# A routing kernel's experts' logits: the rows as stationary operand, and the gate's product in plain float32 in three groups of columns

## The chip, the cores and the metric

The kernel runs on one core of a Trainium2 chip. The metric is the device time of one execution in microseconds (us); each time shown is that of whole executions, and the profile is one further execution. TensorE is called PE in the profile, its weight loads PEld; VectorE is DVE, ScalarE is ACT, GpSimd is POOL, and SyncE, which only issues transfers here, is SP.

## The reference

Three layers follow each other: attention over 4 sequences of 448 rows with 12 heads of 64, a gated feed-forward layer (768 to 1536 and back), and a mixture of 8 experts in which each row goes to one expert.

```python
xn = x / rms * rms_g                      # x: attention's output, 1792 rows of 768
val = (silu(xn @ w_gate) * (xn @ w_val)) @ w_out
logits = val @ moe2_w_gate                # 768 -> 8 experts
# experts are dealt out greedily by logit, 224 rows to each
out[mask_e] = relu(val[mask_e] @ w1[e]) @ w2[e]
```

The order of the logits decides which row goes where, so they are computed in more than one pass of reduced precision, or in plain float32.

## The kernel before

Rows are held in four batches b = 0 to 3 of 448 (four tiles of 112). Two types of product occur. Most are split: an operand is written as a high part and a remainder, both in a reduced float32 format ("fp32r" in the profile), and `mm3` (line 455) issues three products, high by high, high by low, low by high. Plain float32 products take two instructions each on TensorE. All results on TensorE that are not scores land in one ring of four banks, `ffb`.

The program is written as Python generators which are merged by weights (`drv.merge`); a planner then orders each engine's queue with estimated times and the order of writing as priority, and gives out the buffers of each ring. Four stretches follow each other:

1. attention of batch 0 alone, while the feed-forward weights are converted from 64-bit storage and stored back as float32 (`convert`, loads into the buffers `ih`, three of them);
2. attention of later batches merged with the gate and value products of batch 0 (`gateval(0)`), then with the output product of batch 0 (`outproj([0])`) and `gateval(1)`, then with `outproj([1])`, `gateval(2)` and, as a third stream, `gate_rows()` and `gate_done()`;
3. `gateval(3)` with the logits of batch 2;
4. the routing with the output products of batches 2 and 3, then the eight experts.

The parts that the change touches are these.

`x_logits` (line 513) serves batches 0 and 1. For each of the six column blocks j of 128, the output product's block `ot` (128 columns of the row, by 448 rows) has just been copied out of the bank. The logits' gate `wg2t[:, j]` (128 by 8) is the stationary operand and `ot` the moving one, in plain float32; the 8 by 448 result is added into `xl8`, and after the sixth block `xl8` is turned by four transposes and multiplied by the row's 1/rms (`RR`) into `L`. Right after it, `rows_out` turns `ot` itself by four transposes and stores the rows.

`gate_rows` (line 556) serves batches 2 and 3: it makes w_out times the gate, so that their logits can be taken before their output product. For each j and each of three groups c of 512 it loads a 256 KB block `gr` of w_out, turns it by four transposes, splits the result into `wth` (ACT) and `wtl` (DVE), and makes two products with the split gate `wg2s` (both parts side by side, 16 columns) as stationary operand. The 16 by 512 result is added into `wga`, at partitions 32c. `gate_done` turns `wga` and, with `fold`, adds the two parts.

`rms(b)` (line 350) sums the squares `SQ[b]` over columns with four products against a column of ones, in plain float32; DVE scales (line 355) and POOL raises to the power -1/2 (line 356). `rms_rows(b)` (line 358) turns the result over all partitions into `RB`, by which each gate product is multiplied. In `gateval(0)` the first group's twelve steps are sorted by k, since batch 0's last head arrives late; `rms(0)` is called after step 9 and `rms_rows(0)` after step 10.

SP issues the loads of weight pieces (`r_`, line 437), of `ih`, of `gr` (line 561) and the stores `xrow<-xr` (line 536), in one queue.

Of the kernel before, what the change touches and what calls it, by code (L numbers as in the profile page):

```python
# [10 lines left out]
F32 = mybir.dt.float32  # L11
# [19 lines left out]
NI = 3  # L31
# [88 lines left out]
def program(tc, acap, general, qT, kT, v, wf64, g, wg2, w1, w2, out):  # L120
# [4 lines left out]
    with ExitStack() as ctx:  # L125
# [22 lines left out]
            nc.vector.tensor_scalar(gsum, gsum, 1e-9, None, op0=OP.mult)  # L148
        nc.vector.tensor_scalar(gcol, gsum, 1.0 / T, None, op0=OP.mult)
        gt = const.tile([128, KD], F32, name="gt")  # L150
        wg2t = const.tile([128, KD, E], F32, name="wg2t")
        WG = const.tile([128, KF, 2 * E], F32R, name="WG")
        wg2s = const.tile([128, KD, 2 * E], F32R, name="wg2s")
        fold = const.tile([96, E], F32, name="fold")
        L = const.tile([T, NC, E], F32, name="L")
        RR = const.tile([T, B, NQ], F32, name="RR")
# [154 lines left out]

        def gate_constants():
            nc.sync.dma_start(gt, g)
            nc.sync.dma_start(wg2t, wg2)
            nc.vector.tensor_copy(wg2s[:, :, :E], wg2t)
            nc.vector.tensor_tensor(wg2s[:, :, E:], wg2t, wg2s[:, :, :E].bitcast(F32), op=OP.subtract)
            for c in range(3):
                ps = slice(32 * c, 32 * c + 2 * E)
                nc.vector.tensor_tensor(fold[ps], ident[ps, 32 * c:32 * c + E], ident[ps, 32 * c + E:32 * c + 2 * E],
                                        op=OP.add)  # L320

# [138 lines left out]
        def gateval(b):  # L460
            xh, xl = XN[b]
            for f in range(KF):
                z = GV0[b] + f
                split_piece(z + 1)
                wh, wl, r_ = WT.pop(z)
                order = [(j, k) for j in range(2) for k in range(KD)]
                late = b == 0 and f == 0
                if late or (b == B - 2 and f == KF - 1):

                    order.sort(key=lambda jk: jk[1])  # L470
                ps = {}
                for i, (j, k) in enumerate(order):
                    if j not in ps:
                        ps[j] = ff.tile([128, S], F32, name="ffb")
                    mm3(ps[j], wh[:, 6 * j + k], wl[:, 6 * j + k], xh[k], xl[k], k, KD)
                    if f == 0 and i == (2 * KD - 3 if late else 1) and b < B - 1:
                        rms(b)
                    if f == 0 and i == (2 * KD - 2 if late else KD - 1):
                        rms_rows(b)
                    if i % 2:  # L480
                        yield 1.14
                    if (j, k) == (0, KD - 1):
                        o = ps[0]
                        th = ftmp.tile([128, S], F32, name="th", tag="tmp", bufs=3)
                        nc.vector.tensor_tensor(o, o, RB[b], op=OP.mult)
                        nc.scalar.activation(th, o, AF.Tanh, scale=0.5)
                        nc.vector.scalar_tensor_tensor(th, th, 1.0, o, op0=OP.add, op1=OP.mult)  # L487
                pool = tp if b < B - 1 else TP[0]
                th_ = pool.tile([128, S], F32R, name="tfh")
                tl_ = pool.tile([128, S], F32R, name="tfl")  # L490
                TF[b, f] = (th_, tl_)
                nc.vector.scalar_tensor_tensor(th, th, 0.5, ps[1], op0=OP.mult, op1=OP.mult)  # L492
                nc.scalar.activation(th_, th, AF.Copy)  # L493
                nc.gpsimd.tensor_tensor(tl_, th, th_.bitcast(F32), op=OP.subtract)  # L494
# [17 lines left out]

        def x_logits(b, j, ot):

            o = ff.tile([E, S], F32, name="ffb")
            pe.matmul(o, wg2t[:, j], ot, start=True, stop=True)
            if j == 0:
                nc.scalar.activation(xl8, o, AF.Copy)
            else:
                nc.vector.tensor_tensor(xl8, xl8, o, op=OP.add)  # L520
            if j == KD - 1:
                o2 = ff.tile([T, NQ, E], F32, name="ffb")
                for i in range(NQ):
                    pe.transpose(o2[:, i], xl8[:, i * T:(i + 1) * T], ident[96:96 + E, 96:96 + E])
                nc.vector.tensor_tensor(L[:, b * NQ:(b + 1) * NQ], o2, RR[:, b, :, None].to_broadcast([T, NQ, E]),
                                        op=OP.mult)

        def rows_out(b, j, ot):
            if b < B - 2:
# [20 lines left out]
                    drv.later(LAG, partial(rows_out, b, j, ot))  # L550
        C_OP = KD * 6 * 1.14

        wga = const.tile([96 + E, 512], F32, name="wga")
        xl8 = wga[96:, :S]

        def gate_rows():

            for j in range(KD):
                for c in range(3):
                    r_ = wcv.tile([128, 4, 128], F32, name="gr", tag="ih", bufs=NI)  # L560
                    nc.sync.dma_start(r_, wf32[KF + j, :, c * 512:(c + 1) * 512])
                    o = ff.tile([128, 4, 128], F32, name="ffb")
                    for i in range(4):
                        pe.transpose(o[:, i], r_[:, i], ident)
                    th = ftmp.tile([128, 4, 128], F32R, name="wth", tag="xr", bufs=2)
                    tl = ftmp.tile([128, 4, 128], F32R, name="wtl", tag="xr", bufs=2)
                    nc.scalar.activation(th, o, AF.Copy)
                    nc.vector.tensor_tensor(tl, o, th.bitcast(F32), op=OP.subtract)
                    yield 0.5
                    o2 = ff.tile([2 * E, 512], F32, name="ffb")  # L570
                    pe.matmul(o2, wg2s[:, j], th, start=True, stop=False)
                    pe.matmul(o2, wg2s[:, j], tl, start=False, stop=True)
                    d_ = wga[32 * c:32 * c + 2 * E]
                    if j == 0:
                        nc.scalar.activation(d_, o2, AF.Copy)
                    else:
                        nc.vector.tensor_tensor(d_, d_, o2, op=OP.add)
                    yield 0.5

        def gate_done():  # L580
            for c in range(3):
                o = ff.tile([128, 4, E], F32, name="ffb")
                ps = slice(32 * c, 32 * c + 2 * E)
                for i in range(4):
                    pe.matmul(o[:, i], wga[ps, i * 128:(i + 1) * 128], fold[ps], start=True, stop=True)
                wc = WG[:, 4 * c:4 * c + 4]
                nc.vector.tensor_copy(wc[:, :, :E], o)
                nc.vector.tensor_tensor(wc[:, :, E:], o, wc[:, :, :E].bitcast(F32), op=OP.subtract)
            yield 1

        def chain(*gs):
            for gg in gs:
                yield from gg
# [10 lines left out]
        def third():  # L604
            yield from outproj([1])
            yield from gateval(2)
# [7 lines left out]
        split_x(1)  # L614
        drv.merge((islice(att, H), C_ATT), (second(), C_GV + C_OP), (conversion(20), 20))
        split_x(2)
        drv.merge((att, C_ATT), (third(), C_GV + C_OP), (chain(gate_rows(), gate_done()), 19))
        drv.flush()
        actx.close()
        rcon = fctx.enter_context(tc.tile_pool(name="rcon", bufs=1))  # L620
# [387 lines left out]
```

## Time and profile before

| | |
|---|---|
| median of three runs | 1183.07 us (1181.61 to 1188.16) |
| profiled execution, its own time | 1189.33 us |
| its span, first to last instruction | 1187.5 us |
| TensorE busy | 1130.0 us (95%) |
| VectorE busy | 754.1 us (64%) |
| ScalarE busy | 572.6 us (48%) |
| GpSimd busy | 206.8 us (17%) |
| mean granted TensorE clock | 0.975 of full speed |

The profiled execution took 6.3 us more than the median, of which 1.8 us lie outside its span. "Busy" counts an engine's time with an instruction in flight; products on TensorE overlap, so that their durations add up to more than the time that they take, and what a product costs is read from the starts of its neighbours.

### The profile page before, as it was taken

What the parts mean: (1) busy time and instruction counts of PE and PEld (TensorE: products, weight loads), DVE (VectorE), ACT (ScalarE), POOL (GpSimd) and SP (SyncE); (2) the same over time, 40 slices, a digit from 0 to 9 for tenths busy, and PEclk for the clock granted to TensorE, in tenths of its full rate; (3) what the DMA queues carried; (4) which work ended last, traced back from release to release, by engine and by line L of the source; (5) the groups of instructions that cost most, each with busy time, mean ns of one, the idle gap of its engine ahead of it and who ended that gap; (6) DMA issues with size and microseconds to landing.
All of it is one profiled execution on the core that took longest, in us unless ns stands there. A gap on an engine that the chain in (4) does not pass through costs nothing.

```text
span 1187.5 us, 15155 instructions
## 1 busy us (share of the span) xinstructions
PE 1130.0 (95%) x5926; PEld 876.9 (74%) x5926; DVE 754.1 (64%) x1118; ACT 572.6 (48%) x766; POOL 206.8 (17%) x187
## 2 busy tenths in 40 slices
PE   6998999999999999999999999999996999999995
PEld 2335777766587776566778899777775999999995
DVE  4996899998565583555666444255554667666661
ACT  5976657764534564445433233110103565666651
POOL 1222233200022220001112233311101110011000
PEclk8998999999999999999999999999987999999998
DMA  7653465747323333333222233410006666777640
GB/s 253 201 172 131 155 210 190 238 153 261 115 88 103 99 117 94 116 96 107 80 99 80 80 107 107 167 43 24 16 17 192 232 221 235 225 243 228 229 157 26
DMA packets 46114, 169.42 MB, mean 143 GB/s; under 512 B 5424, under 2 KB 16688, under 8 KB 46032
## 3 DMA queue, kind: packets, MB, share of 16 engines
q1 hardware_dynamic: 38896, 142.19, 36.3%
q0 software_dynamic: 7136, 26.16, 6.8%
q8 instruction: 49, 0.80, 0.3%
q14 instruction: 33, 0.27, 0.1%
HBM read 143.16 MB, written 25.17 MB: 142 GB/s over the span
## 4 chain that ended last, share of the span: by engine, by line
PE 74%; issue 10%; DVE 10%; DMA 2%; ACT 1%; POOL 1%; SPq 0%; POOLq 0%; DVEq 0%; ACTq 0%
PE ffb L98 58%; PE l L98 7%; PE ffb L101 3%; PE pb L98 2%; DMA ih<-wf 1%; DVE wl L450 1%; POOL out L932 1%; DVE rc L292 1%; DVE xr L535 0%; DMA mr<-w 0%; POOL RR L356 0%; DVE ps L263 0%; DMA xr<-xrow,idx 0%; DVE xl L376 0%; DVE kc L720 0%
## 5 line engine op out<-in xcount | busy, mean ns | idle before, releaser
L98 PE MATMUL ffb<-xh,wh 128*128 128x448 f32 x576 | 217.8, 378 | 3.1 <-DVE rc L301 2.5
L98 PE MATMUL ffb<-xl,wh 128*128 128x448 f32 x576 | 213.3, 370 | 0.0
L98 PE MATMUL ffb<-xh,wl 128*128 128x448 f32 x576 | 212.8, 370 | 0.0
L841 DVE TENSOR_TENSOR el<-mr,eh 128x1536 fp32r<-128x1536 f32 x64 | 112.5, 1759 | 73.1 <-ACT eh L840 73.1
L494 POOL TENSOR_TENSOR tfl<-th,tfh 128x448 fp32r<-128x448 f32 x48 | 99.7, 2076 | 304.1 <-ACT tfh L493 304.1
L98 PEld LDWEIGHTS ffb<-xh,wh 128*128 128x128 f32 x576 | 109.0, 189 | 32.2 <-issue 9.8
L98 PE MATMUL ffb<-xg,eh 128*128 128x448 f32 x384 | 121.2, 377 | 0.0
L98 PEld LDWEIGHTS ffb<-xl,wh 128*128 128x128 f32 x576 | 109.1, 189 | 11.6 <-issue 2.1
L98 PE MATMUL ffb<-tfh,wh 128*128 128x448 f32 x288 | 117.1, 407 | 0.5 <-DVE th L487 0.5
L98 PEld LDWEIGHTS ffb<-xh,wl 128*128 128x128 f32 x576 | 108.9, 189 | 11.0 <-issue 0.7
L840 ACT ACTIVATE eh<-mr 128x1536 fp32r<-128x1536 f32 x64 | 95.0, 1487 | 30.4 <-PE ffb L98 11.6
L98 PE MATMUL ffb<-tfh,wl 128*128 128x448 f32 x288 | 108.1, 375 | 0.0
L98 PE MATMUL ffb<-tfl,wh 128*128 128x448 f32 x288 | 107.9, 375 | 0.0
L98 PE MATMUL ffb<-xg,el 128*128 128x224 f32 x384 | 92.3, 269 | 0.0
L98 PEld LDWEIGHTS ffb<-xg,el 128*128 128x128 f32 x384 | 74.2, 193 | 1.5
L98 PEld LDWEIGHTS ffb<-xg,eh 128*128 128x128 f32 x384 | 69.5, 191 | 3.8
L98 PEld LDWEIGHTS ffb<-tfh,wh 128*128 128x128 f32 x288 | 56.7, 197 | 15.0 <-issue 7.5
L98 PE MATMUL l<-el,hh 128*112 128x384 f32 x256 | 65.9, 338 | 0.0
L98 PE MATMUL l<-eh,hh 128*112 128x384 f32 x256 | 65.4, 342 | 0.0
L98 PE MATMUL l<-eh,hl 128*112 128x384 f32 x256 | 65.4, 336 | 0.0
L98 PEld LDWEIGHTS ffb<-tfh,wl 128*128 128x128 f32 x288 | 55.6, 193 | 7.0 <-issue 1.4
L492 DVE SCALAR_TENSOR_TENSOR th<-th,ffb 128x448 f32<-128x448 f32 x48 | 29.7, 618 | 47.5 <-PE ffb L98 47.0
(1171 smaller groups left out, 1998.6 us busy)
## 6 DMA issues: line engine op xcount, KB each, us to landing
mr<-w SPq DMA_DIRECT2D x64, 768.0 KB, 4.6
ih<-wf SPq DMA_DIRECT2D x36, 768.0 KB, 5.0
xrow<-xr SPq DMA_DIRECT2D x24, 224.0 KB, 2.5
gr<-wf SPq DMA_DIRECT2D x18, 256.0 KB, 3.6
wf<-r__191 SPq DMA_DIRECT2D x1, 768.0 KB, 5.7
wf<-r__264 SPq DMA_DIRECT2D x1, 768.0 KB, 7.6
wf<-r__341 SPq DMA_DIRECT2D x1, 768.0 KB, 3.5
wf<-r__418 SPq DMA_DIRECT2D x1, 768.0 KB, 3.2
```

The source lines that it names most:

```text
L98: return self.pin(self.tc.nc.tensor.matmul(*a, **k))
L101: return self.pin(self.tc.nc.tensor.transpose(*a, **k))
L292: nc.vector.reciprocal(rc, rc)
L450: eng.tensor_tensor(wl, r_, wh.bitcast(F32), op=OP.subtract)
L492: nc.vector.scalar_tensor_tensor(th, th, 0.5, ps[1], op0=OP.mult, op1=OP.mult)
L494: nc.gpsimd.tensor_tensor(tl_, th, th_.bitcast(F32), op=OP.subtract)
L840: nc.scalar.activation(wh, r_, AF.Copy)
L841: sb = nc.vector.tensor_tensor(wl, r_, wh.bitcast(F32), op=OP.subtract)
L932: st = nc.gpsimd.indirect_dma_start(out=out, out_offset=bass.IndirectOffsetOnAxis(ap=idx[:, 2 * e + t:2 * e + t + 1], axis=0), in_=o_, in_ ...
```

## The change

`x_logits` makes `ot` the stationary operand, in its four tiles of 112 rows, and the gate's 8 columns the moving one; the 112 by 4 by 8 result is added straight into `L`, and `xl8` and its transposes are gone. `gate_rows` loads one 768 KB block per j instead of three of 256 KB, turns it as before, copies the result back over the block in float32 (no split), and then makes three plain float32 products, with the 8 columns of the gate padded by zeros to 32, into three groups of 32 partitions of one bank; one addition of 96 by 512 takes the place of three. The gate is no longer split: `wg2s` is gone, and `wg2t` is set to zero by DVE before its load. `rms(0)` is called after step 6 instead of 9.

```diff
@@ program
-        wg2t = const.tile([128, KD, E], F32, name="wg2t")
+        wg2t = const.tile([128, KD, 32], F32, name="wg2t")
-        wg2s = const.tile([128, KD, 2 * E], F32R, name="wg2s")
@@ gate_constants
-            nc.sync.dma_start(wg2t, wg2)
-            nc.vector.tensor_copy(wg2s[:, :, :E], wg2t)
-            nc.vector.tensor_tensor(wg2s[:, :, E:], wg2t, wg2s[:, :, :E].bitcast(F32), op=OP.subtract)
+            nc.vector.memset(wg2t, 0.0)
+            nc.sync.dma_start(wg2t[:, :, :E], wg2)
@@ gateval
-                    if f == 0 and i == (2 * KD - 3 if late else 1) and b < B - 1:
+                    if f == 0 and i == (KD if late else 1) and b < B - 1:
                         rms(b)
@@ x_logits
-            o = ff.tile([E, S], F32, name="ffb")
-            pe.matmul(o, wg2t[:, j], ot, start=True, stop=True)
+            o = ff.tile([T, NQ, E], F32, name="ffb")
+            for i in range(NQ):
+                pe.matmul(o[:, i], ot[:, i * T:(i + 1) * T], wg2t[:, j, :E], start=True, stop=True)
+            Lb = L[:, b * NQ:(b + 1) * NQ]
             if j == 0:
-                nc.scalar.activation(xl8, o, AF.Copy)
+                nc.vector.tensor_copy(Lb, o)
             else:
-                nc.vector.tensor_tensor(xl8, xl8, o, op=OP.add)
+                nc.vector.tensor_tensor(Lb, Lb, o, op=OP.add)
             if j == KD - 1:
-                o2 = ff.tile([T, NQ, E], F32, name="ffb")
-                for i in range(NQ):
-                    pe.transpose(o2[:, i], xl8[:, i * T:(i + 1) * T], ident[96:96 + E, 96:96 + E])
-                nc.vector.tensor_tensor(L[:, b * NQ:(b + 1) * NQ], o2, RR[:, b, :, None].to_broadcast([T, NQ, E]),
-                                        op=OP.mult)
+                nc.vector.tensor_tensor(Lb, Lb, RR[:, b, :, None].to_broadcast([T, NQ, E]), op=OP.mult)
@@ gate_rows
             for j in range(KD):
+                r_ = wcv.tile([128, 3, 4, 128], F32, name="gr", tag="ih", bufs=NI)
+                nc.sync.dma_start(r_, wf32[KF + j].rearrange("p (c i n) -> p c i n", c=3, i=4))
                 for c in range(3):
-                    r_ = wcv.tile([128, 4, 128], F32, name="gr", tag="ih", bufs=NI)
-                    nc.sync.dma_start(r_, wf32[KF + j, :, c * 512:(c + 1) * 512])
                     o = ff.tile([128, 4, 128], F32, name="ffb")
                     for i in range(4):
-                        pe.transpose(o[:, i], r_[:, i], ident)
-                    th = ftmp.tile([128, 4, 128], F32R, name="wth", tag="xr", bufs=2)
-                    tl = ftmp.tile([128, 4, 128], F32R, name="wtl", tag="xr", bufs=2)
-                    nc.scalar.activation(th, o, AF.Copy)
-                    nc.vector.tensor_tensor(tl, o, th.bitcast(F32), op=OP.subtract)
+                        pe.transpose(o[:, i], r_[:, c, i], ident)
+                    nc.scalar.activation(r_[:, c], o, AF.Copy)
                     yield 0.5
-                    o2 = ff.tile([2 * E, 512], F32, name="ffb")
-                    pe.matmul(o2, wg2s[:, j], th, start=True, stop=False)
-                    pe.matmul(o2, wg2s[:, j], tl, start=False, stop=True)
-                    d_ = wga[32 * c:32 * c + 2 * E]
-                    if j == 0:
-                        nc.scalar.activation(d_, o2, AF.Copy)
-                    else:
-                        nc.vector.tensor_tensor(d_, d_, o2, op=OP.add)
-                    yield 0.5
+                o2 = ff.tile([96, 512], F32, name="ffb")
+                for c in range(3):
+                    pe.matmul(o2[32 * c:32 * c + 32], wg2t[:, j], r_[:, c], start=True, stop=True,
+                              skip_group_check=True)
+                if j == 0:
+                    nc.scalar.activation(wga, o2, AF.Copy)
+                else:
+                    nc.vector.tensor_tensor(wga, wga, o2, op=OP.add)
+                yield 1.0
@@ the third merge: the weight of the gate's stream follows its yields
-        drv.merge((att, C_ATT), (third(), C_GV + C_OP), (chain(gate_rows(), gate_done()), 19))
+        drv.merge((att, C_ATT), (third(), C_GV + C_OP), (chain(gate_rows(), gate_done()), 16))
```

`gate_done` now reads the first 8 partitions of each group of `wga` in place of 16.

## Rows read from the trace of the kernel before

**Rows 1.** The chain that ended last, by engine (shares of the span).

```profile
PE 74%; issue 10%; DVE 10%; DMA 2%; ACT 1%; POOL 1%; SPq 0%; POOLq 0%; DVEq 0%; ACTq 0%
```

**Rows 2.** Busy time in three stretches: window, length, engines, clock, DMA share, GB/s.

```profile
130.00:250.00 120.00, 119.50 (x598) 85.56 (x597) 114.59 (x142) 83.77 (x105) 32.25 (x23) 1.00 0.57 190
250.00:330.00 80.00, 80.00 (x369) 51.94 (x368) 59.27 (x65) 40.01 (x45) 5.51 (x9) 1.00 0.54 179
...
440.00:660.00 220.00, 212.72 (x1036) 155.25 (x1034) 127.48 (x148) 95.46 (x121) 30.59 (x24) 0.99 0.31 99
```

**Rows 3.** TensorE's timeline around an expert-logit product (start us, us, instruction).

```profile
467.28 0.37 PE L98 MATMUL ffb<-tfh,wh 128*128 128x448 f32 x1
467.57 0.92 PE L98 MATMUL ffb<-ot,wg2t 128*8 128x448 f32 x2
468.42 0.47 PE L98 MATMUL ffb<-tfl,wh 128*128 128x448 f32 x1
468.73 0.36 PE L98 MATMUL ffb<-tfh,wl 128*128 128x448 f32 x1
```

**Rows 4.** TensorE's timeline around the sum of squares of batch 2.

```profile
520.58 0.36 PE L98 MATMUL ffb<-xh,wh 128*128 128x448 f32 x1
520.78 0.85 PE L98 MATMUL ffb<-ones,ssq 128*112 128x1 f32 x8
521.50 0.45 PE L98 MATMUL ffb<-xl,wh 128*128 128x448 f32 x1
521.79 0.37 PE L98 MATMUL ffb<-xh,wl 128*128 128x448 f32 x1
```

**Rows 5.** TensorE's timeline, the four transposes of batch 1's summed logits.

```profile
527.19 0.38 PE L101 MATMUL ffb<-ident,wga 8*112 8x8 f32 x4 [0.71 <-DVE wga L520]
```

**Rows 6.** TensorE's timeline, one pair of gate products and its successor.

```profile
612.09 0.39 PE L98 MATMUL ffb<-wth,wg2s 128*16 128x512 f32 x1
...
612.54 0.37 PE L98 MATMUL ffb<-xh,wh 128*128 128x448 f32 x1
```

**Rows 7.** TensorE's timeline, two column halves in plain float32, and their successor.

```profile
487.08 0.97 PE L98 MATMUL ffb<-ps,ones 112*64 112x448 f32 x4
487.98 1.01 PE L98 MATMUL s__3835<-q__3252,k__3253 64*112 64x448 f32 x4
```

**Rows 8.** Timeline of the weight loads, two loads for column halves.

```profile
630.47 0.13 PEld L98 LDWEIGHTS ffb<-t__4522,v__3831 112*64 112x64 f32 x1 [0.31 <-issue]
630.48 0.13 PEld L98 LDWEIGHTS ffb<-t__4523,v__3831 112*64 112x64 f32 x1
```

**Rows 9.** Timeline of all engines, batch 0's sum of squares and its neighbours.

```profile
95.09 0.36 PE L98 MATMUL ffb<-xh,wl 128*128 128x448 f32 x1
...
98.65 0.52 ACT L298 ACTIVATE rc<-ffb 128x448 f32<-128x448 f32 x1
...
99.29 0.95 PE L98 MATMUL ffb<-ones,ssq 128*112 128x1 f32 x8
...
101.95 0.16 DVE L355 TENSOR_SCALAR RR<-ffb 112x4 f32<-112x4 f32 x1
...
102.19 5.30 POOL L356 TENSOR_TENSOR RR<-RR,mhalf 112x4 f32<-112x4 f32 x1 [2.19 <-DVE RR L355]
...
107.54 1.01 PE L101 MATMUL ffb<-ident,RR 112*128 112x112 f32 x4 [5.51 <-POOL RR L356]
```

**Rows 10.** One group of DVE's instructions from 439.4 to 645 us.

```profile
L568 DVE TENSOR_TENSOR wtl<-ffb,wth 128x512 fp32r<-128x512 f32 x18 | 12.3, 681 | 8.1 <-DMA xrow<-xr 4.8 <-ACT wth L567 3.1
```

**Rows 11.** TensorE's waits from 440 to 660 us: total, times, longest.

```profile
PE ffb L98 <- DVE rc L301: 2.5, 1, 2.5
```

**Rows 12.** DVE's timeline at the start, its first conversion.

```profile
16.48 0.56 DVE L409 TENSOR_SCALAR r__191<-ih 128x768 int32<-128x768 int32 x1 [9.85 <-DMA ih<-wf]
```

**Rows 13.** SP's timeline from 440 to 450 us.

```profile
449.88 0.32 SPq L437 DMA_DIRECT2D r__3521<-wf  x1
```

**Rows 14.** DVE's timeline from 484 to 500 us, the split of that piece.

```profile
491.09 1.76 DVE L450 TENSOR_TENSOR wl<-r__3521,wh 128x1536 fp32r<-128x1536 f32 x1
```

More of the change, by code (lines that the diff above doesn't have):

```diff
@@ L313, in gate_constants @@
             nc.sync.dma_start(gt, g)
-            nc.sync.dma_start(wg2t, wg2)
-            nc.vector.tensor_copy(wg2s[:, :, :E], wg2t)
-            nc.vector.tensor_tensor(wg2s[:, :, E:], wg2t, wg2s[:, :, :E].bitcast(F32), op=OP.subtract)
+            nc.vector.memset(wg2t, 0.0)
+            nc.sync.dma_start(wg2t[:, :, :E], wg2)
             for c in range(3):
-                ps = slice(32 * c, 32 * c + 2 * E)
+                ps = slice(32 * c, 32 * c + 32)
                 nc.vector.tensor_tensor(fold[ps], ident[ps, 32 * c:32 * c + E], ident[ps, 32 * c + E:32 * c + 2 * E],
@@ L551, in program @@
         C_OP = KD * 6 * 1.14
-        wga = const.tile([96 + E, 512], F32, name="wga")
-        xl8 = wga[96:, :S]
+        wga = const.tile([96, 512], F32, name="wga")
         def gate_rows():
             for j in range(KD):
+                r_ = wcv.tile([128, 3, 4, 128], F32, name="gr", tag="ih", bufs=NI)
+                nc.sync.dma_start(r_, wf32[KF + j].rearrange("p (c i n) -> p c i n", c=3, i=4))
                 for c in range(3):
-                    r_ = wcv.tile([128, 4, 128], F32, name="gr", tag="ih", bufs=NI)
-                    nc.sync.dma_start(r_, wf32[KF + j, :, c * 512:(c + 1) * 512])
                     o = ff.tile([128, 4, 128], F32, name="ffb")
                     for i in range(4):
-                        pe.transpose(o[:, i], r_[:, i], ident)
-                    th = ftmp.tile([128, 4, 128], F32R, name="wth", tag="xr", bufs=2)
-                    tl = ftmp.tile([128, 4, 128], F32R, name="wtl", tag="xr", bufs=2)
-                    nc.scalar.activation(th, o, AF.Copy)
-                    nc.vector.tensor_tensor(tl, o, th.bitcast(F32), op=OP.subtract)
-                    yield 0.5
-                    o2 = ff.tile([2 * E, 512], F32, name="ffb")
-                    pe.matmul(o2, wg2s[:, j], th, start=True, stop=False)
-                    pe.matmul(o2, wg2s[:, j], tl, start=False, stop=True)
-                    d_ = wga[32 * c:32 * c + 2 * E]
-                    if j == 0:
-                        nc.scalar.activation(d_, o2, AF.Copy)
-                    else:
-                        nc.vector.tensor_tensor(d_, d_, o2, op=OP.add)
-                    yield 0.5
+                        pe.transpose(o[:, i], r_[:, c, i], ident)
+                    nc.scalar.activation(r_[:, c], o, AF.Copy)
+                    yield 0.5
+                o2 = ff.tile([96, 512], F32, name="ffb")
[7 more added lines that the diff above has]
+                yield 1.0
         def gate_done():
@@ L582, in gate_done @@
                 o = ff.tile([128, 4, E], F32, name="ffb")
-                ps = slice(32 * c, 32 * c + 2 * E)
+                ps = slice(32 * c, 32 * c + E)
                 for i in range(4):
```

## The prediction

> **What bounds the kernel.** I read the chain of waits first: TensorE has three quarters of it, and what is called issue is mostly TensorE's own queue [rows 1]. Then busy time by stretch, since the change acts in three places. From 250 to 330 us, where batch 0's expert logits lie, TensorE is never idle; from 440 to 660 us, where batch 1's and all gate products lie, it is idle for 7.3 of 220 us; in both VectorE has slack (59 of 80, 127 of 220). From 130 to 250 us it is otherwise: VectorE is busy for 114.6 of 120 us beside a full TensorE [rows 2]. So time taken from TensorE after 250 us should come off the end nearly one for one, while time won before 130 us may be lost again to VectorE. Last I read TensorE's timeline around each thing that the change replaces. The reader should look at the starts of the neighbours there: split products of 448 columns follow each other at 0.20 us (the first two starts of [rows 4]), and whatever pushes a successor further than that is the price.
>
> **Expert logits, 12 calls.** The product starts 0.29 us after its predecessor, its successor 0.85 us later, and the one after that another 0.31 us later [rows 3]. Against a stream at 0.20 this is 1.14 - 0.20 + 0.11 = 1.05 us, in all 12.6 us. The new form is four products with 112 columns of stationary operand and a moving operand of 8 columns. The trace has the same thing with a moving operand of one column, the sum of squares: also four products, eight instructions, 128 by 112 loads. It takes 0.92 - 0.20 us to its successor and 0.09 us in the next gap, 0.81 us [rows 4]. Twelve of these are 9.7 us, so -2.9 us. Eight columns for one is the unknown. Lower bound: no edges, 0.72 us, -4.0 us. Upper bound: the old price, nothing gained. I take the row, since both are ruled by their loads. Their additions on VectorE become shorter (32 elements instead of 448) and were not in TensorE's way, except once.
>
> **Transposes of the sum.** After the sixth block four transposes of 0.38 us stood in TensorE's queue, twice, and batch 1's waited 0.71 us for VectorE's addition [rows 5]. Both go, with the bank that they used; the new multiplication of `L` follows on VectorE alone, with nobody behind it but the routing, 200 us later. About 0.2 us each for the transposes (they overlap with neighbours) and the wait: -1.1 us; bounds 0 and -1.5.
>
> **Gate products.** Before, 18 pairs at 0.45 us to the successor [rows 6], 8.1 us. After, six rounds of three plain float32 products of 512 columns. One such product of 448 takes 0.85 us [rows 3], so 0.97 us at 512. Do three run side by side? Two column halves of 64 in plain float32, four instructions, take 0.90 us to their successor [rows 7], against 0.85 for a single product: the second half costs 0.05. Their weight loads start 10 ns apart [rows 8]. With two more groups at 0.05 and the edges of 0.20 (0.09 and 0.11, as above), a round is 0.97 + 0.10 + 0.20 = 1.27 us, six are 7.6: -0.5 us. Bounds: no edges, 6.4 us, -1.7; one after the other, 3 x 0.97 + 0.20 = 3.1 us a round, 18.7 us, +10.6. I take the side-by-side price, which the halves are nearest to.
>
> A rule speaks against this. The Trainium skill ("TensorE: Matmul & The Clock Gate", Part 3, The mechanism) has a weight load overlap with matmuls in flight only when the row group differs; column groups share their rows. By that rule the three groups would run one after the other. By the halves' rows it doesn't hold for two groups of 64; no run here shows three of 32.
>
> The 72 transposes and their copies on ACT stay. VectorE loses 18 subtractions, 12.3 us [rows 10], and ten additions of like width, so near 19 us of work, off the path where TensorE has other products to run. In this stretch TensorE waited 2.5 us behind a reciprocal, before which VectorE still had one of these additions to do [rows 11], and there are a few shorter waits. I count -1.0 us; bounds 0 and -4.
>
> **Squares of batch 0.** The four products ran at 99.29 and were over by 100.24 us, VectorE's scaling came at 101.95, POOL's power took 5.30 us from 102.19, and TensorE stood still for 5.51 us until the transposes at 107.54 [rows 9]. The call moves up by three steps, nine products or 1.8 us of stream. But the last of the group's 36 products had already started at 95.09 us, so what the squares waited for wasn't their place in the program. They run right after ACT has emptied a bank of the ring of four, at 98.65 + 0.52 us [rows 9], which head 6 of the attention had taken before them in either order. So I expect them no earlier. What the move can change is the place of the scaling on VectorE, 1.7 us after its input was ready, behind pieces of weight conversion, one of which is now written after it. I take this: -1.7 us. Bounds: 0 (VectorE loses the gain again before 250 us) and -5.5 (all of the stall). If the squares were queued too early for their bank, TensorE would stand before the rest of the group's products, and those would then fill POOL's 5.3 us, so that little is lost.
>
> **The rest.** SP's load of `wg2t` now waits for VectorE's clearing, and behind it stand the next loads of weights. VectorE is idle for 9.85 us before its first conversion at 16.48 us [rows 12], so the clearing lies there and costs nothing; without that cover it would be an instruction of some 0.2 us. The load is cut into 32-byte pieces, but nobody reads it before the expert logits, after 250 us. Two short instructions on VectorE leave the start-up. 0, bounds -1 and +1. The loads of `gr` have the same bytes in 6 instead of 18 issues.
>
> **Sum.** -2.9 - 1.1 - 0.5 - 1.0 - 1.7 = -7.2 us. From the profiled execution's 1189.33 this gives 1182.1. That execution was 6.3 us above the median of 1183.07, most of it inside the span, and I have no row that says where, so the forecast is the median less the sum: 1176 us. About 0.5%, 5.9 us, is what a measurement here can tell from no change.
>
> **Rivals.**
> 1. *The squares come early after all*: the planner gives them their bank before head 6 takes it, and POOL's power runs under products. For it: the group's last products use head 5's block, as the squares do, so at 95.09 us their data can't have been far [rows 9]. Against: head 6 is written first. -5.5 in place of -1.7: 1172 us.
> 2. *Nothing but the cheap parts.* Eight moving columns cost more than one, the squares stay where they are, VectorE's relief hits nobody: -1.7 (a logit call at 0.91, with the 0.10 by which the squares' longer record exceeds the shorter one [rows 4, 9]), -0.5 and no more: 1181 us. For it: TensorE's idle time is small, and it is waits of other kinds.
> 3. *The three groups run one after the other*: +10.6 for -0.5, the rest as forecast: 1187 us. Against it are the halves.
> 4. *Slower: SP's queue is held by `gr`.* A buffer now stays taken for a whole round, up to 220 / 6 = 37 us, instead of one step. SP waits in order: its weight pieces are issued behind `gr`, as `r__3521` was at 449.88 [rows 13]. Three of the six loads need a buffer given back. The cover is that this piece is used at 491.09, 41 us after its issue [rows 14]. Each hold above 41 us costs TensorE the excess; three holds of 45 us or more turn -7 into more than +5.9, and three of 50 us give 1176 + 27 = 1203 us. Against it: a hold should not outlast a round, and a round is shorter than the cover.
>
> **Chances.** The forecast has 0.48, with a range of its own of 1170 to 1181, cut at 1177.2 by the bound for faster: 0.34 faster, 0.14 the same. Rival 1: 0.17, faster. Rival 2: 0.18, the same. Rival 3: 0.10, of which 0.07 the same and 0.03 slower. Rival 4: 0.07, slower. So faster 0.51, same 0.39, slower 0.10. The range goes from 1166 (rival 1 with the lower bound of the logits and of VectorE's waits) to 1187 (rival 3), leaving out rival 4, half of rival 3 and the far ends.
>
> **What would show it.** Right: successors of an expert-logit call start about 0.9 us after it is queued instead of 1.14; six rounds of `wga` products whose successors start about 1.1 us after them; no transposes of 8 by 8; VectorE busy about 20 us less from 440 to 660 us; the squares of batch 0 still behind a bank, their scaling directly after them. Wrong: rounds of 3 us; a squares' product before 95 us; SP waiting tens of microseconds at line 561's successor while TensorE waits for a weight piece; or a change in a stretch that nothing here touches, which would mean that the planner dealt the queues anew.

## The result, and the profile after

The changed kernel takes 1167.71 us (median of four runs, 1167.17 to 1170.78) against 1184.55 (1181.61 to 1188.16) for the kernel before on the same chip: a ratio of 0.984 [0.982, 0.987]. The medians differ by 16.8 us; the ratio on record isn't quite that of the two medians and stands for 18.7 us [15.5, 21.9]. The time lies inside the predicted range, near its lower end, but the forecast movement was 7.2 us: the direction was right and the size was off by more than a factor of two. The profiled execution took 1167.32 us, with a span of 1165.3, 22.2 us under that of before; but the profiled execution of before stood 4.8 us above its median, so these 22.2 us are more than the change is worth.

Where the time came off is read first from milestones that both traces have: the moment at which the work reaches the same instruction.

```
us from the start of the span                    before   after   difference
transposes of batch 0's 1/rms (PE, RR)            107.5   104.8    -2.7
last group of gateval(0)      (POOL, tfl)         248.4   243.2    -5.2
outproj([0]), sixth block     (ACT, ot)           313.7   305.1    -8.6
last group of gateval(1)      (POOL, tfl)         437.1   428.2    -8.9
outproj([1]), sixth block     (ACT, ot)           516.9   500.3   -16.6
first group of gateval(3)     (POOL, tfl)         664.6   647.1   -17.5
last group of gateval(3)      (POOL, tfl)         754.5   735.4   -19.1
end of the span                                  1187.5  1165.3   -22.2
```

The gain grows nearly everywhere, and also where nothing was edited. The last 3.1 us of it go with TensorE's granted clock: over 755 to 860 us it was 0.95 before, and over 736 to 841, which is about the same work, 0.98 after (1.00 is the higher of its two levels, 2.4 GHz; products of 448 columns are 0.20 us apart there and 0.37 at the lower one, 1.2 GHz). But `gateval(3)` is 1.6 us shorter, and there the clock is full in both. That stretch is the cleanest piece of the trace, since TensorE runs 376 split products there with nothing between them. Its timeline after, with the first and the last step of that run (start us, us, instruction):

```profile
654.89 0.37 PE L98 MATMUL ffb<-xl,wh 128*128 128x448 f32 x1
655.09 0.37 PE L98 MATMUL ffb<-xh,wl 128*128 128x448 f32 x1
...
729.90 0.36 PE L98 MATMUL ffb<-xl,wh 128*128 128x448 f32 x1
730.10 0.36 PE L98 MATMUL ffb<-xh,wl 128*128 128x448 f32 x1
```

and the same run in the kernel before:

```profile
671.97 0.37 PE L98 MATMUL ffb<-xl,wh 128*128 128x448 f32 x1
672.17 0.37 PE L98 MATMUL ffb<-xh,wl 128*128 128x448 f32 x1
...
748.96 0.37 PE L98 MATMUL ffb<-xl,wh 128*128 128x448 f32 x1
749.16 0.37 PE L98 MATMUL ffb<-xh,wl 128*128 128x448 f32 x1
```

376 steps take 77.19 us before and 75.21 after: 205.3 and 200.0 ns a step, at the full granted clock in both. A single row, printed to 0.01 us, hides this; the difference shows only over many. The same products, unedited, have become faster. Over the whole trace (the mean over some 1,500 of the 1,728 gate and value products, those that follow each other directly) the pace is 205.3 ns before and 200.9 after, so 1,728 x 4.4 ns = 7.6 us.

Busy time of the kernel after in the three stretches of [rows 2]:

```profile
130.00:250.00 120.00, 118.67 (x600) 87.09 (x599) 115.97 (x141) 79.95 (x101) 31.73 (x23) 1.00 0.56 190
250.00:330.00 80.00, 80.00 (x411) 57.75 (x411) 55.23 (x66) 40.66 (x45) 7.44 (x10) 1.00 0.62 208
440.00:660.00 220.00, 220.00 (x1106) 160.77 (x1105) 106.83 (x127) 95.90 (x119) 32.46 (x25) 1.00 0.28 92
```

From 440 to 660 us (the same window, though the work in it stands 9 to 17 us further on) VectorE is busy 20.7 us less, as forecast; but TensorE's 7.3 us of idle time are gone altogether (220.00 of 220), where the sum had counted on 1.0. The new instructions stand on TensorE's timeline like this. An expert-logit call after (it answers to [rows 3]):

```profile
262.89 0.36 PE L98 MATMUL ffb<-tfl,wh 128*128 128x448 f32 x1
263.09 0.86 PE L98 MATMUL ffb<-wg2t,ot 128*112 128x8 f32 x8
263.81 0.63 PE L101 MATMUL ffb<-ident,ot 128*112 128x128 f32 x4
```

Its successor starts 0.72 us after it; in the twelve calls this is 0.71 to 0.88 (seven of them at 0.71 or 0.72, all seven behind a split product), where the price of before was 0.85 with gaps of 0.09 and 0.11 around it. Two rounds of gate products after (they answer to [rows 6]); the second was dealt out in two pieces, four and two of its six instructions:

```profile
450.21 0.36 PE L98 MATMUL ffb<-tfh,wh 128*128 128x448 f32 x1
450.50 1.06 PE L98 MATMUL ffb<-gr,wg2t 128*32 128x512 f32 x6
451.49 0.47 PE L98 MATMUL ffb<-tfl,wh 128*128 128x448 f32 x1
...
524.42 1.05 PE L98 MATMUL ffb<-gr,wg2t 128*32 128x512 f32 x4
525.40 0.47 PE L98 MATMUL ffb<-xl,wh 128*128 128x448 f32 x1
...
527.85 1.05 PE L98 MATMUL ffb<-gr,wg2t 128*32 128x512 f32 x2
528.83 0.47 PE L98 MATMUL ffb<-xh,wh 128*128 128x448 f32 x1
```

This is the measurement of the side-by-side question. Three groups push their successor by 0.99 us, two by 0.98, one by 0.98: the second and the third group cost nothing that can be seen. A whole round with its edges is 0.09 + 0.99 + 0.11 = 1.19 us.

Batch 0's squares after, from the timeline of all engines (it answers to [rows 9]):

```profile
98.68 0.53 ACT L298 ACTIVATE rc<-ffb 128x448 f32<-128x448 f32 x1
...
99.30 0.95 PE L98 MATMUL ffb<-ones,ssq 128*112 128x1 f32 x8
...
101.50 0.15 DVE L354 TENSOR_SCALAR RR<-ffb 112x4 f32<-112x4 f32 x1
101.74 3.02 POOL L355 TENSOR_TENSOR RR<-RR,mhalf 112x4 f32<-112x4 f32 x1 [1.72 <-DVE RR L354]
...
104.82 0.60 PE L101 MATMUL ffb<-ident,RR 112*128 112x112 f32 x4 [2.76 <-POOL RR L355]
```

The squares stand where they stood (99.30 against 99.29), behind the same bank. VectorE's scaling comes 0.45 us earlier; what is new is POOL's power, 3.02 us for 5.30, and with it TensorE's stall, 2.76 for 5.51.

Whole executions of one and the same kernel differ by their mean granted clock. The 53 executions of the kernel before that are on record reach from 1191.77 us at a clock of 0.975 to 1179.77 at 0.985; fitted within each kernel over all 115 executions here, a thousandth of clock goes with 0.9 us. The four of the changed kernel had 0.981 to 0.984, in the mean 0.983, and those of before 0.979. At one and the same clock the change is therefore worth an estimated 14.7 us, [13.4, 16.0], and not 16.8 or 18.7. How much of the clock is the kernel's own doing the runs don't part; the estimates at one clock below have this open end too.

### The profile page after: what moved, and what is told of

Same layout as the page of the kernel before. It is cut to its first block, busy times and chain, and to the rows that moved or that the text cites. A ratio compares the mean times of both kernels' runs of the same rounds, so it can differ in the third digit from the quotient of the medians.

```text
span 1165.3 us, 15198 instructions
## 1 busy us (share of the span) xinstructions
PE 1114.6 (96%) x5990; PEld 876.9 (75%) x5990; DVE 728.4 (63%) x1091; ACT 571.2 (49%) x762; POOL 203.2 (17%) x187
## 5 line engine op out<-in xcount | busy, mean ns | idle before, releaser
L98 PE MATMUL ffb<-xh,wh 128*128 128x448 f32 x576 | 214.7, 373 | 0.3 <-DVE th L486 0.3
L98 PE MATMUL ffb<-xl,wh 128*128 128x448 f32 x576 | 209.8, 364 | 0.0
L98 PE MATMUL ffb<-xh,wl 128*128 128x448 f32 x576 | 209.6, 364 | 0.0
L485 ACT ACTIVATE th<-ffb 128x448 f32<-128x448 f32 x48 | 26.0, 542 | 71.3 <-DVE ffb L484 71.2
```

The source lines that it names most:

```text
L98: return self.pin(self.tc.nc.tensor.matmul(*a, **k))
```

## The experiments

Three explanations were open: (a) the edited instructions and the waits that they empty; (b) the places of the buffers, since the new `wg2t` has 768 bytes a partition where `wg2t` and `wg2s` had 576 together, so that everything placed behind them on that side of the memory, the weight pieces `wh` and `wl` among them, lies 192 bytes higher, while the split rows `xh` and `xl`, on the other side, stay (by the sizes and the order in which the kernels ask for their buffers); (c) the chip or the hour. Ratios are to the kernel before on the same chip, with a 95% interval; a run without one is a single execution, and single executions of the kernel before ranged from 1180 to 1192 us. "At one clock" marks an estimate by the 0.9 us of the section before, with a 95% interval or its half-width after +-.

**The kernel before, once more.**

> The kernel before once more, unchanged. If the 205 ns from start to start of the gate and value products and POOL's 5.3 us power belong to the program, both are seen again (205 ns within 1, power above 5 us, TensorE idle about 5.5 us before batch 0's turned rms). If they belong to that one execution, they differ: 200 to 203 ns, or a power of 1 to 4 us.

Measured: 1186.24 us, 205.3 ns a step, the power 5.29 us. Pace, power and stall belong to the program, not to the one execution; for these three (c) is out. For the granted clock it isn't.

**The places alone.** The kernel before, with one unused tile ahead of the others:

```diff
+        shift = const.tile([128, 48], F32, name="shift")
+        nc.vector.memset(shift, 0.0)
```

> Kernel before with one unused tile of 192 bytes per partition among the constants, so that every buffer behind it (the split weights among them) lies 192 bytes further, where the changed kernel has it, while the split rows xh, xl stay. No instruction of the change. Theory of places: the gate and value products start every 200 to 202 ns in place of 205, and the time falls by 4 to 9 us. Theory of the parts (the gain comes from the instructions removed): 205 ns as before, 0 us (within 2).

Measured: 1178.03 us, ratio 0.9926 [0.9908, 0.9945], 8.8 us less, with no instruction of the computation touched. Its pace is 201.2 ns. The page's groups of these products (busy us, mean ns) for the shifted kernel:

```profile
L98 PE MATMUL ffb<-xl,wh 128*128 128x448 f32 x576 | 210.8, 366 | 0.0
L98 PE MATMUL ffb<-xh,wl 128*128 128x448 f32 x576 | 210.1, 365 | 0.0
```

and for the kernel before:

```profile
L98 PE MATMUL ffb<-xl,wh 128*128 128x448 f32 x576 | 213.3, 370 | 0.0
L98 PE MATMUL ffb<-xh,wl 128*128 128x448 f32 x576 | 212.8, 370 | 0.0
```

1,728 x 4.1 ns = 7.1 us, and at one clock the run is 7.2 us [6.2, 8.3] faster than the kernel before: the pace accounts for it. The power took 2.56 us in this run, but that need not add to the time; the run of the squares below shows how little of it lasts.

**All of the change at the old places.** The gate's columns packed into the room of `wg2s`, so that nothing behind it moves; the stationary operand of a group then has the next columns where the change has zeros, in rows of the result that nobody reads:

```diff
+        wg2t = const.tile([128, KD, E], F32, name="wg2t")
+        wg2f = const.tile([128, 96], F32, name="wg2f")
...
+                    pe.matmul(o2[32 * c:32 * c + 32], wg2f[:, E * j:E * j + 32], r_[:, c], start=True, stop=True,
+                              skip_group_check=True)
```

> Changed kernel with its padded gate packed into the room of the old split gate (groups overlap in 72 columns, the surplus results are not read), so that all buffers lie where the kernel before has them; all instructions of the change are there. Theory of places: 205 ns again, and 4 to 9 us more than the changed kernel, so 8 to 13 us under the kernel before. Theory of the parts: 200 to 202 ns and the full 17 us.

Measured: 1176.11 us, ratio 0.9909 [0.9892, 0.9926]: 10.8 us of the change by the ratio are its instructions and the waits that they empty, and the other 8.0 of 18.7 appear only with the new places. At one clock it is 8.0 us and 6.6, +- 1.1 and 1.6. Either way the places are not far from half. The pace is back at 205.3 ns, and TensorE is still never idle from 440 to 660 us.

**The squares alone.**

```diff
-                    if f == 0 and i == (2 * KD - 3 if late else 1) and b < B - 1:
+                    if f == 0 and i == (KD if late else 1) and b < B - 1:
```

> Kernel before with only the call of rms(0) moved from step 9 to step 6. In the queues that run, only VectorE's scaling moves, one instruction of 0.55 us earlier. Theory of the order: POOL's power falls from 5.3 to about 3.0 us, TensorE's wait from 5.5 to about 2.8, and the time by 3 to 5 us. Rival (that power's length is chance of an execution): 0.5 us or nothing.

Measured: 1185.39 us, ratio 0.9981 [0.9967, 0.9995]. Against the kernel before, the only reordering up to the stall is that the scaling trades places with one instruction of weight conversion (line 409), as the prediction had it; the power then took 3.03 us and the stall 2.77. The 2.0 us won at the transposes (105.5 for 107.5) still stood at the end of `outproj([0])` (311.7 for 313.7); they were 0.4 at the end of `outproj([1])` and 0.5 when `gateval(3)` ended. TensorE's idle 7.3 us between 440 and 660 remained (212.71 busy). So the gain at the stall is seen, and most of it is lost again; what is left at the end is 2.2 us [0.6, 3.9] by the ratio, 0.7 between the medians and 0.7 [-0.1, 1.4] at one clock, which is not told from nothing.

**The expert logits alone** (the edit of `x_logits`, nothing else).

> Kernel before with only the experts' logits taken with the rows as stationary operand; all buffers at the places of the kernel before. By the sum's term (0.24 us a call and the transposes): -3 to -4 us, spacing of the products 205 ns, TensorE's idle time of about 7 us from 440 to 660 us unchanged. Rival (that idle time comes from the additions of 8 by 448 in VectorE's queue): the idle time shrinks by several us and the time by 6 to 10.

Measured: 1179.71 us, ratio 0.9952 [0.9934, 0.997], 5.7 us less, at 205.3 ns a step. The three longest of TensorE's five waits from 440 to 660 us in this kernel (total, times, longest):

```profile
PE ffb L98 <- DVE rc L301: 2.5, 1, 2.5
PE s__4542 L98 <- ACT t__4402 L219: 1.0, 1, 1.0
PE ffb L98 <- ACT RB L364: 0.6, 1, 0.6
```

The wait for the sum's addition (0.7 [rows 5]) is gone with the transposes, and so is one of 1.7 for `oT`; that behind the reciprocal [rows 11] remains. The power took 2.56 us here, though no line near it was edited.

**The gate's product alone** (`gate_rows`, `gate_done`, `gate_constants` and the weight of its stream, at the old places).

> Kernel before with only the gate's product in plain float32 in three groups of columns, buffers at the places of the kernel before. By the sum's terms (-0.5 and -1.0): -1 to -2 us, TensorE still idle for some 6 us from 440 to 660 us. Rival (VectorE's 28 instructions fewer empty the waits): TensorE idle under 1 us there, -5 to -8 us. Either way 205 ns from start to start.

Measured: 1177.35 us, ratio 0.994 [0.9919, 0.996], 7.1 us less, at 205.3 ns a step. Its stretch from 440 to 660 us:

```profile
440.00:660.00 220.00, 220.00 (x1077) 156.84 (x1076) 110.66 (x124) 98.10 (x123) 31.61 (x25) 1.00 0.28 94
```

This edit by itself empties all of TensorE's idle time there; VectorE falls from 127.48 to 110.66 us. Power and stall were those of before (5.29 and 5.51), so nothing of this gain comes from them. Here one round of the six was dealt out in two pieces, not two: seven insertions in place of the 18 pairs. The three parts add up to 15.0 us alone and 10.8 together (13.0 and 8.0 at one clock). Two overlaps are seen: the 2.3 us of waits that the logits remove are among those that the gate removes, and the power is shortened by the squares' move and by the logits, but only once. That they make up the whole difference isn't shown.

**Which places?** Five kernels. The kernel after with the feed-forward's rows `tfh` and `tfl` moved 96 bytes down as well:

> Changed kernel, its padded gate packed into 72 columns, and two unused tiles that leave the split weights where they are and put the output products' split rows tfh, tfl of batches 0 to 2 96 bytes lower, at the distance from the weights (160 or 416 modulo 512) at which xh, xl lie in the changed kernel. No other instruction of weight. If that distance sets the pace: their products go from 203.6 to 200 or 201 ns, the gate and value products stay at 201, and the time falls by 1 to 3 us below the changed kernel. If it is the weights' or the rows' own place or chance: 203.6 ns, no change (within 1 us).

The kernel before with 64, 128 and 256 bytes in place of the 192 above:

> As the shift by 192 bytes, but by 64: the split rows lie 288 and 32 bytes (modulo 512) behind the weights instead of 352 and 96 before and 160 and 416 at 192. If any shift does it: 200 to 202 ns. If the pace depends on the distance: another value between 200 and 206 ns, and the time moves by about 1.3 us for each nanosecond.

> The kernel before with one unused 128-byte tile per partition, so that the weight pieces and all buffers on their side lie 128 bytes higher while the split rows stay. Theory (the pace of the split products is set by where the operands lie): the pace of the products xh, xl by wh, wl differs from 205.3 ns; the trend of +64 bytes (204.3) and +192 bytes (201.2) would give 202 to 204, and a time of 1178 to 1184 us. Rival (the pace goes with the run or the chip, and +192 bytes met it by chance): 205.3 ns, 1184 to 1188 us.

> The kernel before with an unused tile of 256 bytes. Theory that the places count by their rest in 256 bytes: the pace is that of before, 205.3 ns, and the time 1184 to 1188 us. Rival (other rests, or the distance as such): a pace away from 205.3 by over 0.5 ns, with a time 1 us off for each 0.6 ns.

The kernel after with the gate packed and its neighbours 128 bytes above their old places:

> The kernel after, with the gate's columns packed as in the run with the old places and an unused tile, so that the buffers of that side lie 128 bytes higher than before instead of 192. All instructions are those of the change. If the pace at this place lies between those at 64 and 192 bytes (204.3 and 201.2 ns): 1170 to 1174 us, slower than the kernel after by 2 to 6 us. If this place is better than the change's own for the feed-forward output products as well (203.6 ns there): 1163 to 1167 us, which would beat it.

And the kernel before with the 192 unused bytes on the other side, under the rows, so that the weights stay:

```diff
+        padr = xctx.enter_context(tc.tile_pool(name="padr", bufs=1, side="right")).tile([128, 48], F32, name="padr")
+        nc.vector.memset(padr, 0.0)
         oTp = xctx.enter_context(tc.tile_pool(name="oT", bufs=1, side="right"))
```

> The kernel before with an unused 192-byte tile on the other side of the memory: the split rows lie 192 bytes lower, and weights, conversion buffers and all else on their side stay where they were. The distance from weights to rows is thus that of the kernel after, by moving the other operand. Theory that the distance sets the pace: 201 ns instead of 205.3, and 1175 to 1181 us. Rival (the place of the weights by itself): 205.3 ns, 1183 to 1188 us.

Measured, with the mean pace of the products of `xh`, `xl` and of those of `tfh`, `tfl` by the weights:

```
                                  weights to rows,   pace, ns      time, us                                less than before
                                  against before     x     tf                                              at one clock, us
before                              0               205.3 203.8    1184.6 to 1186.1 (medians)              0
before, weights 64 bytes higher    -64              204.3 203.3    1181.24 (one)                           2.4 +- 2.4
before, weights 128 higher         -128             204.2 203.6    1184.25 (one)                           3.8 +- 2.4
before, weights 192 higher         -192             201.2 203.9    1178.03, 0.9926 [0.9908, 0.9945]        7.2 +- 1.0
before, weights 256 higher         -256             205.4 204.1    1190.01 (one)                          -0.2 +- 2.5
before, rows 192 lower             -192             200.6 203.9    1178.26, 0.9935 [0.991, 0.996]          6.6 +- 0.9
change, old places                  0               205.3 204.3    1176.11, 0.9909 [0.9892, 0.9926]        8.0 +- 1.1
change, weights 128 higher         -128             204.1 203.9    1172.35, 0.9902 [0.9879, 0.9925]       10.2 +- 1.1
change                             -192             200.9 203.6    1167.71, 0.9842 [0.9815, 0.9869]       14.7 +- 1.3
change, tf rows 96 lower           -192             201.0 202.4    1169.44, 0.9874 [0.9855, 0.9893]       15.2 +- 1.1
```

The page's group of the products of `xl` by `wh` in two of these runs, first with the rows 192 bytes lower, then with the weights 256 higher (for the kernel before it is 213.3, 370):

```profile
L98 PE MATMUL ffb<-xl,wh 128*128 128x448 f32 x576 | 211.0, 366 | 0.0
```

```profile
L98 PE MATMUL ffb<-xl,wh 128*128 128x448 f32 x576 | 213.3, 370 | 0.0
```

Three rows decide. Moving the rows down does what moving the weights up does (200.6 and 201.2), so it is a distance between the two sides of the memory that counts, not the place of either side; and the power stayed at 5.29 us in that run, so its gain doesn't come from the stall. That the distance is the one between the two operands of a product is shown by the last row: the feed-forward rows lie on the weights' side and move with them, so that their distance is the same in all kernels but this one, and so is their pace (203.3 to 204.3). Where they alone are moved it is 202.4, while that of `xh` and `xl` stays. The mean over all of them hides most of it: the move concerns batches 0 to 2, and of the directly following steps in batches 0 and 1, 250 of 377 are of 200 ns there, against 21 of 377 in the kernel after. And 256 bytes bring the old pace back (205.4), so what was tried agrees with a period of 256 bytes. Of the single times, +128 and +256 came out just above what was expected of them, at granted clocks of 0.977 and 0.975. In time no variant is told from the kernel after: 128 bytes are slower (1172.35), and 1.2 ns on 864 feed-forward products, 1.0 us, are too little to be seen.

## Why the prediction was right or wrong

**What failed first is the step called "The rest"**, 0 with bounds of -1 and +1. It followed the changed buffers' loads and clearing and never asked what their size does to the addresses behind them. That is worth 8.0 us (0.9842 against 0.9909), or 6.6 at one clock, near half of the gain, and the shifted kernel shows it with none of the edits, 0.9926. The pace says the same: 4.4 ns on 1,728 products are 7.6 us. The prediction's row of 0.20 us for a split product was read from single starts at two decimals; 5 ns were below its grain. Its own last sentence named a change in a stretch that nothing touches as a sign of error, and blamed the planner for it beforehand; the sign came, `gateval(3)`, and the cause was another.

**VectorE's relief**, -1.0 with a bound of -4: mis-sized, and the second step that failed. The waits of 440 to 660 us were 7.3 us and all went. The row behind the reciprocal [rows 11] was read rightly, as an addition of the gate standing ahead of it on VectorE: it stays when the logits alone change and goes when the gate changes. Treating the others as "shorter waits" of other kinds was wrong, since the gate's edit empties them too. That the ACT waits among them go through VectorE is only argued: with a new gate stream the planner's order in this stretch is new as well, and the runs don't part the two.

**Gate products**, -0.5: wrong in sign, by little. The price of a round was 1.19 us against 1.27 forecast, so the halves were the right neighbour. But two of the six rounds were dealt out in two pieces, each at the full 0.98: eight insertions x 1.19 = 9.5 us against 18 x 0.45 = 8.1, +1.4 us (in the run with the gate alone it is seven, 8.3 us, +0.2). The edit wins through the waits, not on TensorE's products. Rival 3 is out: by the rows after, one, two and three column groups over the same rows push the successor by 0.98, 0.98 and 0.99 us. With the rule of the Trainium skill ("TensorE: Matmul & The Clock Gate", Part 3, The mechanism), by which a weight load overlaps with matmuls in flight only when the row group differs, the prediction made 3.1 us a round of it; these rows, with 1.19, don't agree. The same Part 3 also lists a gain for three column tiles, which the prediction passed over.

**Expert logits and their transposes**, -2.9 - 1.1: right in the price of a call, which pushes its successor by 0.71 or 0.72 us in seven of twelve cases, where 0.72 with 0.09 of edge was forecast. The edit alone gave 5.7 us [3.6, 7.8], 6.1 at one clock; 2.3 of idle time in 440 to 660 us (212.72 to 214.98 busy) are in that, 0.7 of them the named wait, and transposes of `RR` that come 2.1 us earlier (105.4), which the squares' run shows to be mostly lost again. The interval takes in the forecast 4.0 without resolving its parts; the wait of 1.7 us for `oT`, which goes as well, wasn't in the forecast.

**Squares of batch 0**, -1.7 with bounds 0 and -5.5: the place was right, no earlier than the bank, and rival 1 is out. The size isn't resolved: alone it is 2.2 us [0.6, 3.9] by the ratio but 0.7 between the medians and at one clock, and by the milestones 0.5 of the 2.0 us lasted; if it came near 1.7, that is luck, since the mechanism was half right at most. The scaling moved by 0.45 us, not by 1.7; the stall shrank because POOL's power got shorter, which no step had foreseen. The same power takes 1.03 or 1.04 us in batches 1 and 2 of both traces; in batch 1 of before, VectorE pauses for 4.24 us after its scaling. Here it took 5.30, 3.02 or 2.56 us. In the kernel before, VectorE's timeline beside it:

```profile
102.02 0.95 DVE L413 SCALAR_TENSOR_TENSOR r__806<-ih,r__806 128x768 int32<-128x768 int32 x1
102.89 0.95 DVE L412 SCALAR_TENSOR_TENSOR r__688<-ih,r__688 128x768 int32<-128x768 int32 x1
103.75 1.09 DVE L263 TENSOR_TENSOR ps<-ps,t__788 112x896 f32<-112x896 f32 x1
104.76 0.95 DVE L413 SCALAR_TENSOR_TENSOR r__688<-ih,r__688 128x768 int32<-128x768 int32 x1
105.62 0.95 DVE L414 SCALAR_TENSOR_TENSOR r__806<-u__807,r__806 128x768 f32<-128x768 bf16 x1
```

Instructions with two inputs follow each other without a gap until 106.57, and the power ends at 107.49, 0.92 after them. In the kernel with the logits alone:

```profile
102.76 2.56 POOL L356 TENSOR_TENSOR RR<-RR,mhalf 112x4 f32<-112x4 f32 x1 [2.18 <-DVE RR L355]
...
103.46 0.95 DVE L412 SCALAR_TENSOR_TENSOR r__688<-ih,r__688 128x768 int32<-128x768 int32 x1
104.33 1.08 DVE L263 TENSOR_TENSOR ps<-ps,t__788 112x896 f32<-112x896 f32 x1
105.33 0.95 DVE L413 SCALAR_TENSOR_TENSOR r__688<-ih,r__688 128x768 int32<-128x768 int32 x1
```

the power ends at 105.32, where one such instruction gives way to the next. This looks as if it were held up by VectorE's stream and slipped through at a seam or after the last instruction; why at this seam and not at an earlier one, no row says. The Trainium skill ("SBUF — State Buffer", Who interferes with whom) has VectorE and GpSimd share a port pair as a lock, taken against GpSimd's reads by a VectorE instruction with two inputs in SBUF, the on-chip memory of the buffers; the rows agree, but no run here took VectorE's stream away, so the cause stays argued.

Behind the long stall stands a second price, which the prediction left out. Before, the granted clock over 84 to 112 us was 0.88, with products 0.37 us apart in the trace from 108.75 to 111.36; after it was 1.00 and they stay at 0.20. Of all 14 traces here, the five with the long stall had 0.88, 0.88, 0.88, 0.90 and 0.94 over these 28 us, the nine with the short one 0.94 or 1.00. The 2.5 us wait of 440 to 660 us shows the same once: TensorE resumes at 568.05, and from 569.07 to 571.68 its products are 0.37 us apart. The clock over that stretch is 0.99 in the kernel before and 1.00 in the change, at its own and at the old places, and in the gate alone; but two more variants of the change without any wait there have 0.99, so an emptied wait isn't all that the clock follows.

**Rival 4** is out: TensorE has no wait at all in 440 to 660 us, and the page's row for `gr` shows 5.2 us from issue to landing, as `ih` had before with the same bytes (5.0):

```profile
gr<-wf SPq DMA_DIRECT2D x6, 768.0 KB, 5.2
```

Its own sum was off by a little: three holds of 45 us cost 12 us, which turns -7.2 into +4.8 and not into more than +5.9.

**The frame.** The medians differ by 16.8 us and the profiled executions by 22.0 (1189.33 and 1167.32), so the 6.3 us by which the one of before stood above its median didn't belong to the kernel, and the forecast rightly started from the median. All of them lie inside its span, since the other executions have about 1.8 us outside theirs too; and they go with its granted clock, 0.975, at which the seven executions of that kernel took 1189.1 to 1191.8 us. That the measured time lies inside the range is luck. The low end was put there for rival 1, which didn't happen, and it is lower than its own terms: with the lower bounds of the logits (-4.0) and of VectorE's waits (-4) rival 1 gives 1168.0 us, not 1166, and 1167.71 lies under that. The two terms that were sized wrong, the places and VectorE's waits, both lay on the faster side.

## What to carry to other kernels

When a change alters the size of any buffer, ask what lies behind it: compare the pace of untouched products over hundreds of steps before crediting the edit, and measure the edit at the old addresses and the addresses without the edit. Set the granted clocks of the executions beside their times: here they make 2 us of the 16.8. For a stream that is off the bound, count the waits that it causes on TensorE's timeline, all of them, before its own instructions: with the gate's edit alone the products cost 0.2 us more, and the kernel was 7.1 us faster. Don't price a short GpSimd instruction on the path by its length elsewhere alone: look at what VectorE runs beside it.

## What the runs showed of the hardware that was not expected

The pace of back-to-back split products on TensorE depended on the distance between the stationary and the moving operand in the memory: 205.3, 204.3, 204.2, 201.2 and again 205.4 ns with the weights 0, 64, 128, 192 and 256 bytes higher, and 200.6 with the rows 192 lower; over 376 undisturbed steps 205.3 and 200.0. For the feed-forward rows it was 203.3 to 204.3 ns at one distance and 202.4 at the only other one tried, at which two thirds of the steps in batches 0 and 1 are of 200 ns; by the expectation of that run its remainder by 256 is that at which the other products take 201.0. Why a distance matters, why the two sets differ, and whether the period is 256, for which one run speaks, is open; no run here looks inside a product.

One power of 112 by 4 on GpSimd took 1.03 us beside a pausing VectorE and up to 5.30 beside a busy one, within one trace.

Plain float32 products of 128 by 32 with 512 columns, in one, two and three groups of columns over the same rows, pushed their successor on TensorE by 0.98, 0.98 and 0.99 us.
